# Linear attention and a gated layer on one core: key sums folded into the attention weights before the division, the division one unit later, key sums on VectorE, weight scans spread over the first layer

## The chip, the cores and the metric

The kernel runs on one core of one Trainium2 chip. The metric is device time in microseconds (us), the median of a kernel's runs. The program uses one core, so there is no second die to compare with; every run quoted here was listed as fast, with a granted TensorE clock between 0.99 and 1.00. The engines are called as the profile calls them: PE is TensorE, PEld its weight loads, DVE is VectorE, ACT is ScalarE, POOL is GpSimd, SP is SyncE, which here only issues transfers.

## The reference, cut to what matters

```python
def _A_ref(x, wqkv, wo):                 # linear attention, 32 heads of 32, S = 2048, D = 1024
    qkv = (x @ wqkv)...                  # q, k, v per head (reshape cut)
    phi = lambda t: jnp.where(t > 0, t + 1, jnp.exp(t)) + 1e-6
    pq, pk = phi(q), phi(k)
    kv  = jnp.einsum("bhsd,bhse->bhde", pk, v)
    z   = jnp.einsum("bhsd->bhd", pk)                             # the key sums
    num = jnp.einsum("bhqd,bhde->bhqe", pq, kv)
    den = jnp.einsum("bhqd,bhd->bhq", pq, z)[..., None] + 1e-6
    return (num / den)... @ wo                                    # (reshape cut)

def _B_ref(x, w_gate, w_up, w_down):     # gated layer, F = 3584
    return ((x @ w_gate) * (x @ w_up)) @ w_down                   # (written with einsum)

x = A_x                                  # bf16
x = x + _A_ref(_layernorm(x), ...)       # attention layer 1
x = x + _B_ref(_layernorm(x), ...)       # gated layer 1
x = x + _A_ref(_layernorm(x), ...)       # attention layer 2, the same weights
x = x + _B_ref(_layernorm(x), ...)       # gated layer 2, the same weights
```

## The kernel before

The attention layer never forms v. It computes phi(k) for all 16 row tiles (the **K stage**), then the 16 products of the normalised input with phi(k) (`xk_unit`, "X by K"), then multiplies them with the value weights (the **key-value product**, `kv_unit`), and folds the result with the output weights (`kvo_unit`, the **fold**). Each query tile (`q_unit`) goes through phi, is divided by its denominator on VectorE, is transposed by a DMA, and is multiplied with the folded matrix (`out_unit`, the **output stage**).

The gated layers work in fp16, and their weights are scaled by powers of two. The scale of each weight matrix comes from the sum of its squares. ScalarE takes these sums in 42 **scans** of 512 KB each, all of them hidden in the first attention layer: a DMA brings a piece, and ScalarE squares it in place with an accumulator.

The parts that matter (cuts marked `...`):

```python
    pqb = [W[:, i * D:(i + 1) * D] for i in range(3)]        # three buffers for phi(q) of a tile
    pb = [W[:, 6 * D + i * NB:6 * D + (i + 1) * NB] for i in range(4)]   # phi's biased copy x1
    scan_b = [W[:, 6 * D:8 * D], ...]                        # scan buffers; this one is the memory of pb
    ...
    EARLY, MID = 30, 39
    scanned = [0, 0, EARLY]         # scans done, fetched, allowed to be fetched

    def mm_tile():                  # the next of 8 PSUM banks
        count["mm"] = count.get("mm", -1) + 1
        return Q[count["mm"] % 8]

    def over_den(t):                # the division of tile t
        pq = pqs.pop(t)
        nc.vector.tensor_tensor(out=prod, in0=pq, in1=zb, op=ALU.mult)          # prod, zb: fp32
        den = small.tile([P, NH], F32, tag="den", name="den")
        nc.vector.tensor_reduce(out=den[:], in_=prod..., axis=AX.X, op=ALU.add)
        ...                                                                     # + 1e-6, reciprocal
        nc.vector.tensor_tensor(out=pqh, in0=pqh, in1=den..., op=ALU.mult)
        tx(pq, t, t // TPG)                                                     # transpose by DMA

    def kvo_unit(c, n):             # one piece of the fold
        ps = mm_tile()
        nc.tensor.matmul(out=ps, lhsT=kvt[:, c, :], rhs=wo[n][:, c, :], start=True, stop=True)
        nc.scalar.copy(out=KVo[n][:, c, :], in_=ps)

    def layer_A(li):
        sks = [sum_unit(t, nc.gpsimd if li == 0 and t < 9 else nc.vector) for t in range(1, NT)]
        ...
            for i, (t, n) in enumerate(units):                # first layer: the K stage
                u = k_mm(t, n)                                # (one special case cut)
                ...
                phi(*u)
                for x in late:
                    norm(x)                                   # normalise and transpose later tiles
                if i == 4:
                    scan_fetch()                              # four 512 KB loads at once
                if i >= 8 and i % 2 == 0:
                    scans()
                if 18 <= i < 26:
                    do(sks[:1])                               # eight key sums on GpSimd
                    sks = sks[1:]
        ...
        first = 5 if li == 0 else 4
        per = -(-len(sks) // (first - 3))
        for i in range(first):                                # the first X-by-K products
            xk[i]()
            do(sks[per * i:per * (i + 1)])                    # the other key sums, VectorE
            scans()
            if i == first - 3:
                z_parts()
        ...
        XT_ = 8
        for t in range(XT_):                                  # 16 Q units woven with the other products
            q[2 * t](); ...; q[2 * t + 1](); ...; scans(2 if t < 6 else 1)      # and 22 scans
        load_o()                                              # output weights, on SyncE's queue
        kv_unit()
        ...                                                   # Q 16-22 with the fold, Q 23-31 with outputs
```

## Time and profile before

The kernel took 1522.84 us as the median of three runs, and 1523.14 us (1521.97 to 1526.46) as the median of four. The top of the profile page gives the busy time of each engine, and its fourth part the shares of the chain of work that ended last.

```profile
PE 1490.2 (98%) x6995; PEld 677.9 (45%) x6995; DVE 1075.2 (71%) x1804; ACT 744.6 (49%) x934; POOL 87.3 (6%) x195
...
PE 86%; ACT 6%; DVE 3%; DMA 3%; issue 1%; SPq 1%; POOL 0%; ACTq 0%; DVEq 0%
```

TensorE bounds the kernel. What can be won without taking away matmuls is the time in which TensorE waits, or runs with a cold (halved) clock after a wait. The table of windows shows where that is. Each row is one stretch: its limits and length, the busy time and instruction count of PE, PEld, DVE, ACT and POOL, the granted clock, the DMA share and GB/s. The rows end at the end of the first X-by-K product, the start of the key-value product, its end, the end of the output stage, and then gated layer 1, attention layer 2 and gated layer 2.

```profile
0.00:81.73 81.73, 68.80 (x318) 29.95 (x318) 62.00 (x118) 55.67 (x72) 34.10 (x65) 0.97 0.84 220
81.73:163.36 81.63, 81.63 (x374) 36.75 (x372) 50.82 (x69) 65.35 (x81) 0.00 (x0) 0.98 0.73 205
163.36:169.41 6.05, 3.89 (x65) 3.65 (x64) 5.66 (x10) 5.49 (x7) 0.00 (x0) 1.00 0.66 180
169.41:265.13 95.72, 88.88 (x405) 39.60 (x403) 76.98 (x135) 59.02 (x90) 14.10 (x34) 0.98 0.59 140
265.13:779.12 513.99, 509.45 (x2353) 230.47 (x2352) 371.53 (x641) 236.14 (x262) 16.00 (x38) 1.00 0.51 150
779.12:1008.75 229.63, 229.38 (x1109) 105.73 (x1108) 172.20 (x284) 105.89 (x173) 16.24 (x43) 1.00 0.33 76
1008.75:1520.80 512.05, 508.19 (x2381) 231.73 (x2379) 336.01 (x551) 217.02 (x250) 6.90 (x16) 1.00 0.38 115
```

Attention layer 2 is busy for 229.38 of its 229.63 us. Attention layer 1 does the same work and adds the scans and the start; nearly all holes lie there or, with 4.0 us, at the start of the gated layer that follows it. The waits of PE name them (line of the waiting matmul, what it waited for, its line; total us, how often, the longest):

```profile
PE Q L338 <- DMA K<-ST: 4.8, 1, 4.8
PE Q L353 <- DVE K L328: 4.7, 2, 3.3
PE Q L501 <- DVE X L425: 4.0, 1, 4.0
PE Q L421 <- DMA TX<-in_A_wo_dram: 3.2, 1, 3.2
PE Q L413 <- ACT K L355: 2.2, 2, 1.9
PE Q L338 <- DVE part L233: 2.1, 1, 2.1
PE Q L421 <- DMA ST<-in_A_wo_dram: 1.3, 1, 1.3
```

(Q is PSUM, the eight banks into which TensorE writes its results; X is the activation x; K, W, MX, TX, ST and XT are buffers that the kernel reuses for many things.) L338 is the matmul of a K or Q projection, L353 that of an X-by-K product, L413 the key-value product, L421 the fold, L501 the gated layer's matmul. So, in this order: a transposed tile of the input arrives late in the K stage; the first product waits for the last phi(k) from VectorE; the first gated matmul waits for the last additions to x; the output weights arrive late; the key-value product waits for ScalarE's copies; a bank is read late by VectorE; and once more the output weights.

Why is VectorE late with phi(k)? The timeline of VectorE and GpSimd around 62 to 74 us shows it (start, duration in us, engine, line, operation, shapes):

```profile
63.21 10.96 POOL L361 TENSOR_TENSOR K<-K,K 128x1024 f32<-128x1024 f32 x5
...
67.42 0.29 DVE L327 TENSOR_SCALAR W<-W 128x512 bf16<-128x512 bf16 x1 [1.21 <-ACT W L326]
68.35 1.55 DVE L327 TENSOR_SCALAR W<-W 128x512 bf16<-128x512 bf16 x1
```

The same clamp of phi takes 0.29 us, or 1.55 us when it starts in the middle of a key sum of GpSimd (2.12 us each; the five are merged into one line above). In narrower windows one sum ends at 67.55 us, just after the short clamp has started, and the next runs from 67.63 to 69.76 us: the long clamp ends right after it, at 69.90 us. The Trainium skill, "SBUF — State Buffer", section "SBUF: two separate sides", says that VectorE in its two-port modes and GpSimd share a port pair that is held for a whole instruction. The trace agrees with that.

### The profile page before, as it was taken

Reading aid. Unit: us, or ns where it says so; the run is one execution under the profiler, and the core shown is the slowest. Engines: PE = TensorE matmul, PEld = TensorE weight load, DVE = VectorE, ACT = ScalarE, POOL = GpSimd, SP = SyncE. Lnnn points to the kernel's source line nnn. Section 1 sums busy time; section 2 is a strip of 40 time slices with the busy share of each in tenths; the row PEclk is TensorE's granted clock in tenths of the full one; section 3 lists DMA queues with packets and bytes.
Section 4 is the critical chain, followed back from the end, with each engine's and each line's share of the span. In section 5 each row is a group of like instructions: output and inputs, shape, how many; then the busy total and the mean of one; then the engine's idle time right before and its main releaser. Section 6 shows DMA issues by size and latency. Waiting matters only on the chain.

```text
span 1520.8 us, 18444 instructions
## 1 busy us (share of the span) xinstructions
PE 1490.2 (98%) x6995; PEld 677.9 (45%) x6995; DVE 1075.2 (71%) x1804; ACT 744.6 (49%) x934; POOL 87.3 (6%) x195
## 2 busy tenths in 40 slices
PE   9889899999999999999999999999999999999998
PEld 3334444444444444444444444444444444444444
DVE  7767786888867577776578667867776746777533
ACT  4978656677720266660013336576664015666300
POOL 3500002000001000000010000110000100000000
PEclk9999999999999999999999999999999999999999
DMA  7967827576658322334851014152323664322342
GB/s 220 209 199 200 256 46 172 154 209 198 197 189 221 92 84 83 84 104 157 238 133 40 15 32 117 33 139 84 83 84 125 184 193 115 84 83 83 146 169 80
DMA packets 277049, 202.78 MB, mean 133 GB/s; under 512 B 102113, under 2 KB 264161, under 8 KB 273377
## 3 DMA queue, kind: packets, MB, share of 16 engines
q1 hardware_dynamic: 265760, 186.94, 43.8%
q10 hardware_dynamic: 11200, 14.68, 3.1%
q8 instruction: 54, 0.88, 0.2%
q14 instruction: 35, 0.28, 0.1%
HBM read 160.43 MB, written 17.04 MB: 117 GB/s over the span
## 4 chain that ended last, share of the span: by engine, by line
PE 86%; ACT 6%; DVE 3%; DMA 3%; issue 1%; SPq 1%; POOL 0%; ACTq 0%; DVEq 0%
PE Q L501 45%; PE Q L786 22%; PE Q L338 8%; PE Q L433 5%; PE Q L353 5%; ACT K L217 2%; ACT W L326 1%; DVE W L327 1%; DVE K L328 1%; DMA TX<-in_A_wo_dram 1%; DMA K<-in_B_w_up_dram 1%; DMA X<-in_A_x_dram 1%; ACT K L422 0%; DMA K<-in_B_w_gate_dram 0%; DMA W<-in_B_w_down_dram 0%
## 5 line engine op out<-in xcount | busy, mean ns | idle before, releaser
L501 PEld LDWEIGHTS <-K 128*128 128x128 f16 x3136 | 307.2, 98 | 376.2 <-issue 7.4
L501 PE MATMUL Q<-XT,K 128*128 128x512 bf16 (+1 forms) x1792 | 407.2, 380 | 4.0 <-DVE X L425 4.0
L786 PE MATMUL Q<-K,K 128*128 128x512 f16 (+1 forms) x1596 | 340.8, 375 | 1.0 <-DVE X L793 1.0
L501 PE MATMUL Q<-TX,K 128*128 128x512 f16 x1344 | 308.3, 379 | 0.5 <-ACT MX L523 0.5
L463 ACT ACTIVATE K<-K,fac 128x2048 f16<-128x2048 bf16 x112 | 218.3, 1999 | 127.9 <-DMA K<-in_B_w_gate_dram 127.0
L786 PEld LDWEIGHTS <-K 128*128 128x128 f16 x1596 | 155.1, 98 | 185.0 <-issue 1.3
L466 DVE TENSOR_TENSOR K<-K 128x1024 f16<-128x1024 f16 (+1 forms) x244 | 157.2, 666 | 37.2 <-ACT K L463 35.3
L466 DVE TENSOR_TENSOR W<-MX,Q 128x512 f16<-128x512 f32 x176 | 116.5, 684 | 30.4 <-ACT MX L523 18.0
L338 PE MATMUL Q<-K,K 128*128 128x512 bf16 x512 | 117.3, 385 | 6.9 <-DMA K<-ST 4.8
L326 ACT ACTIVATE W<-Q 128x512 bf16<-128x512 f32 x90 | 53.0, 596 | 140.2 <-PE Q L338 124.6
L523 ACT COPY MX<-Q 128x512 f32<-128x512 f32 x120 | 69.2, 585 | 96.5 <-PE Q L501 96.5
L338 PE MATMUL Q<-K,XT 128*128 128x512 bf16 x512 | 114.6, 379 | 1.3 <-ACT XT L314 0.7
L466 DVE TENSOR_TENSOR W<-W,Q 128x512 f16<-128x512 f32 x160 | 105.6, 683 | 11.4 <-ACT W L523 4.9
L523 ACT COPY W<-Q 128x512 f32<-128x512 f32 x104 | 60.3, 585 | 73.0 <-PE Q L501 73.0
L466 DVE TENSOR_TENSOR K<-K,K 128x512 f16<-128x512 f16 (+1 forms) x148 | 87.6, 597 | 4.2
L466 DVE TENSOR_TENSOR K<-W,Q 128x512 f16<-128x512 f16 x56 | 38.4, 686 | 72.9 <-PE Q L501 72.8
L338 PEld LDWEIGHTS <-K 128*128 128x128 bf16 x512 | 50.5, 99 | 69.6 <-issue 7.0
L793 DVE SCALAR_TENSOR_TENSOR W<-Q,kap,X 128x512 f32<-128x512 f32 x32 | 24.0, 750 | 77.6 <-PE Q L786 77.6
L338 PEld LDWEIGHTS <-XT 128*128 128x128 bf16 x512 | 49.6, 98 | 61.5 <-ACT XT L314 1.5
L505 DVE TENSOR_TENSOR K<-W 128x512 f16<-128x512 f16 x168 | 71.3, 425 | 5.8
L217 ACT ACTIVATE K<-K 128x2048 bf16<-128x2048 bf16 x36 | 69.0, 1918 | 6.8 <-DMA K<-in_B_w_down_dram 3.2
L327 DVE TENSOR_SCALAR W<-W 128x512 bf16<-128x512 bf16 x90 | 33.3, 370 | 47.2 <-ACT W L326 47.1
(109 smaller groups left out, 1264.3 us busy)
## 6 DMA issues: line engine op xcount, KB each, us to landing
K<-WD SPq DMA_DIRECT2D x28, 1792.0 KB, 7.3
K<-in_B_w_gate_dram SPq DMA_DIRECT2D x70, 512.0 KB, 4.0
K<-in_B_w_up_dram SPq DMA_DIRECT2D x56, 512.0 KB, 5.1
K<-in_A_wqkv_dram SPq DMA_DIRECT2D x10, 1024.0 KB, 8.3
K<-in_B_w_up_dram ACTq DMA_DIRECT2D x14, 512.0 KB, 3.8
K<-in_B_w_down_dram SPq DMA_DIRECT2D x10, 512.0 KB, 5.3
WD<-K SPq DMA_DIRECT2D x10, 512.0 KB, 3.0
X<-in_A_x_dram SPq DMA_DIRECT2D x16, 256.0 KB, 5.3
```

The source lines that it names most:

```text
L217: nc.scalar.activation(out=scan_buf[i], in_=scan_buf[i], func=ACT.Square, accum_out=acc[:, m, c:c + 1])
L326: nc.scalar.activation(out=e, in_=ps, func=ACT.Exp)
L327: nc.vector.tensor_scalar(out=e, in0=e, scalar1=1.0, scalar2=1e-6, op0=ALU.min, op1=ALU.add)
L338: nc.tensor.matmul(out=ps, lhsT=xt[:, k, tl * P:(tl + 1) * P], rhs=w[:, k, :], start=(k == 0), stop=(k == KD - 1))
L353: nc.tensor.matmul(out=ps, lhsT=xn_a[t][:, j * P:(j + 1) * P], rhs=pk[t][:, n * NB:(n + 1) * NB], start=(t == 0), stop=(t == NT - 1))
L433: nc.tensor.matmul(out=ps, lhsT=xT[t // TPG][:, c, tl * P:(tl + 1) * P], rhs=KVo[n][:, c, :], start=(c == 0), stop=(c == KD - 1))
L463: nc.scalar.activation(out=b.bitcast(F16), in_=b, func=ACT.Copy, scale=fac[:, m:m + 1])
L466: eng.tensor_tensor(out=o, in0=a, in1=b, op=op)
L501: nc.tensor.matmul(out=pair[m], lhsT=stationary(n, p, m, k), rhs=moving[p][:, k, :], start=(p in (1, 2, 5) and k == 0), stop=(k == KH - 1) ...
L505: nc.vector.tensor_tensor(out=hA[i][:, u, :], in0=gu[:, 0, :], in1=gu[:, 1, :], op=ALU.mult)
L523: nc.scalar.copy(out=snaps[u, p][:, m, :], in_=a[m])
L786: nc.tensor.matmul(out=ps_[:, lo:hi], lhsT=act[:, u, j * P:(j + 1) * P], rhs=w[:, u, lo:hi], start=(p in (1, 2, 5) and u == 0), stop=(u == ...
```

## The change

Its intent, as the diff shows it:

- **Algebra.** The key sums are multiplied into phi(q) in place (phi(q) times z). The row sums of that product are the denominators, and the same product goes on to the division and the output. The fold takes the factor out again: ScalarE scales each row of the folded matrix by 1/z (`z_column` makes z a column and takes its reciprocal). The key sums become bf16, and the divided tiles fp16.
- **Deferral.** The division of a tile no longer follows its phi at once. Its first half follows the phi of the next Q unit, its second half the phi after that.
- **Key sums on VectorE.** All 15 of them, three behind each of the first five X-by-K products; before, eight were on GpSimd.
- **Scans spread.** Their loads no longer start four at a time; the K stage has 7 scans instead of 11.
- **Order.** Ten instead of eight pairs of Q units before the key-value product; the output weights are loaded from ScalarE's queue; the fold uses banks 5 to 7, while everything else in that stretch rotates over banks 0 to 4; two additions at the end of the layer go ahead of the row statistics; the last tile of the program is cut differently.

The diff, cut to its core:

```diff
-    prod, zb = (MX[:, 2 * D * i:2 * D * (i + 1)].bitcast(F32) for i in range(2))
+    zb = MX[:, 0:D]
@@
-            load(wo[n], wo_v[:, :, n * NB:(n + 1) * NB])
+            nc.scalar.dma_start(out=wo[n], in_=wo_v[:, :, n * NB:(n + 1) * NB])
@@
-    EARLY, MID = 30, 39
+    EARLY, MID = 32, 36
     ... (scan buffers regrouped)
-    scanned = [0, 0, EARLY]
+    scanned = [0, 0, 0]
@@
-    def mm_tile():
+    def mm_tile(narrow=[8]):
         count["mm"] = count.get("mm", -1) + 1
-        return Q[count["mm"] % 8]
+        return Q[count["mm"] % narrow[0]]
+    rotation = mm_tile.__defaults__[0]
@@ q_unit
             phi(proj_mm(t, wq[n]), pqs[t][:, n * NB:(n + 1) * NB], split)
+            flush()                              # the oldest deferred half, if there is one
             if n == 1:
-                over_den(t)
+                later[:] = over_den(t)           # [sums, divide]
@@ the division
-        nc.vector.tensor_tensor(out=prod, in0=pq, in1=zb, op=ALU.mult)
+        nc.vector.tensor_tensor(out=pq, in0=pq, in1=zb, op=ALU.mult)
     ...
-        nc.vector.tensor_tensor(out=pqh, in0=pqh, in1=den..., op=ALU.mult)
+        nc.vector.tensor_tensor(out=pqh.bitcast(F16), in0=pqh, in1=den..., op=ALU.mult)
@@ kvo_unit
-        ps = mm_tile()
+        ps = turn("kvo", Q[5:8])
     ...
-        nc.scalar.copy(out=KVo[n][:, c, :], in_=ps)
+        nc.scalar.activation(out=KVo[n][:, c, :], in_=ps, func=ACT.Copy, scale=rz[:, c:c + 1])
@@ layer_A
-        sks = [sum_unit(t, nc.gpsimd if li == 0 and t < 9 else nc.vector) for t in range(1, NT)]
+        sks = [sum_unit(t, nc.vector) for t in range(1, NT)]
@@
-                if i == 4:
+                if i >= 5 and i % 2:
+                    scanned[2] = (i - 3) // 2 if i < len(units) - 1 else EARLY
                     scan_fetch()
-                if i >= 8 and i % 2 == 0:
+                if 10 <= i <= 22 and i % 2 == 0:
                     scans()
-                if 18 <= i < 26:
-                    do(sks[:1])
-                    sks = sks[1:]
@@
-        XT_ = 8
+        XT_ = 10
     ... (the order of scans, fold, outputs and norms in the output stage)
+        rotation[0] = 5
+        for i in range(6):
+            q[22 + i]()
+            do(kvo[8 * i // 3:8 * (i + 1) // 3])
+            if i > 2:
+                out_next()
+        rotation[0] = 8
+        for i in range(4):
+            q[28 + i]()
+            out_next(2)
```

More of the change, by code (lines that the diff above doesn't have):

```diff
@@ L109 @@
     scan_b = [W[:, 6 * D:8 * D], K[0][:, HEAD:HEAD + 2 * D]]
-    scan_c = scan_b + [K[i][:, HEAD:HEAD + 2 * D] for i in (4, 5)]
+    scan_c = [K[i][:, HEAD:HEAD + 2 * D] for i in (4, 0)]
     xn_c = {TPG + i: tail(i, 0) for i in range(4)}
@@ L196 @@
     NSCAN = 3 * NU
-    EARLY, MID = 30, 39
-    scan_buf = [scan_a[i % 4] for i in range(EARLY)] + [scan_b[i % 2] for i in range(MID - EARLY)]
-    scan_buf += [scan_c[i % 4] for i in range(NSCAN - MID)]
-    scanned = [0, 0, EARLY]
+    EARLY, MID = 32, 36
+    scan_buf = [scan_a[i % 4] for i in range(18)] + [(scan_a + scan_b[:1])[i % 5] for i in range(18, EARLY)]
+    scan_buf += [scan_b[(i + 1) % 2] for i in range(MID - EARLY)] + [scan_c[i % 2] for i in range(NSCAN - MID)]
+    scanned = [0, 0, 0]
     def scan_fetch():
@@ L381, in z_unit, with z_column @@
             nc.scalar.copy(out=zb[:, n * NB:(n + 1) * NB], in_=ps)
+    rz = const.tile([P, KD], F32, tag="rz", name="rz")
+    def z_column():
+        ps = mm_tile()
+        for c in range(KD):
+            nc.tensor.matmul(out=ps[:, c:c + 1], lhsT=zb[:, c * P:(c + 1) * P], rhs=ident[:, 0:1], start=True, stop=True)
+        nc.vector.reciprocal(out=rz[:], in_=ps[:, 0:KD])
     pqs = {}
@@ L389, in run, with flush, den_sums, den_divide @@
             phi(proj_mm(t, wq[n]), pqs[t][:, n * NB:(n + 1) * NB], split)
+            flush()
             if n == 1:
-                over_den(t)
+                later[:] = over_den(t)
         return run
+    later = []
+    def flush():
+        if later:
+            later.pop(0)()
     def over_den(t):
         pq = pqs.pop(t)
-        nc.vector.tensor_tensor(out=prod, in0=pq, in1=zb, op=ALU.mult)
         den = small.tile([P, NH], F32, tag="den", name="den")
-        nc.vector.tensor_reduce(out=den[:], in_=prod.rearrange("p (h e) -> p h e", e=32), axis=AX.X, op=ALU.add)
+        return [lambda: den_sums(pq, den), lambda: den_divide(t, pq, den)]
+    def den_sums(pq, den):
+        nc.vector.tensor_tensor(out=pq, in0=pq, in1=zb, op=ALU.mult)
+        nc.vector.tensor_reduce(out=den[:], in_=pq.rearrange("p (h e) -> p h e", e=32), axis=AX.X, op=ALU.add)
         nc.vector.tensor_scalar(out=den[:], in0=den[:], scalar1=1e-6, scalar2=None, op0=ALU.add)
         nc.vector.reciprocal(out=den[:], in_=den[:])
+    def den_divide(t, pq, den):
         pqh = pq.rearrange("p (h e) -> p h e", e=32)
-        nc.vector.tensor_tensor(out=pqh, in0=pqh, in1=den[:].unsqueeze(2).to_broadcast([P, NH, 32]), op=ALU.mult)
+        nc.vector.tensor_tensor(out=pqh.bitcast(F16), in0=pqh, in1=den[:].unsqueeze(2).to_broadcast([P, NH, 32]),
+                                op=ALU.mult)
         tx(pq, t, t // TPG)
@@ L432, in run @@
             for c in range(KD):
-                nc.tensor.matmul(out=ps, lhsT=xT[t // TPG][:, c, tl * P:(tl + 1) * P], rhs=KVo[n][:, c, :],
+                nc.tensor.matmul(out=ps, lhsT=xT[t // TPG][:, c, tl * P:(tl + 1) * P].bitcast(F16), rhs=KVo[n][:, c, :],
                                  start=(c == 0), stop=(c == KD - 1))
@@ L605, in norm_act @@
         return out_
+    sums_t = []
     def layer_A(li):
         k = [k_unit(t, n) for t in range(NT) for n in range(2)]
-        sks = [sum_unit(t, nc.gpsimd if li == 0 and t < 9 else nc.vector) for t in range(1, NT)]
+        sks = [sum_unit(t, nc.vector) for t in range(1, NT)]
         first_A = li == 0
@@ L680, in layer_A @@
         q = [q_unit(t, n, li > 0 or t > 12) for t in range(NT) for n in range(2)]
-        first = 5 if li == 0 else 4
-        per = -(-len(sks) // (first - 3))
+        first = 6 if li == 0 else 4
+        per = -(-len(sks) // (first - (0 if first_A else 2)))
         for i in range(first):
@@ L685, in layer_A @@
             do(sks[per * i:per * (i + 1)])
-            scans()
-            if i == first - 3:
+            if i == first - (1 if first_A else 2):
                 z_parts()
+            scans(2 if i < 3 else 1)
         rest = xk[first:]
-        XT_ = 8
+        XT_ = 10
         for t in range(XT_):
             q[2 * t]()
+            scans()
+            do(rest[len(rest) * t // XT_:len(rest) * (t + 1) // XT_])
             if t == 0:
                 z_unit()
-            scans()
+            elif t == 2:
+                z_column()
+            elif first_A and t == 7:
+                scale_sum(0, 2)
+            elif first_A and t == 8:
+                scale_pow(0, 2)
             q[2 * t + 1]()
-            do(rest[len(rest) * t // XT_:len(rest) * (t + 1) // XT_])
-            scans(2 if t < 6 else 1)
+            if t < 8:
+                scans()
         load_o()
@@ L701, in layer_A @@
         load_unit(0, 0)
-        if first_A:
-            scale_sum(0, 2)
-        for i in range(4):
-            q[16 + i]()
-            if i == 2:
-                scanned[2] = NSCAN
-                scans()
-        kvo = [lambda c=c: kvo_unit(c // 2, c % 2) for c in range(2 * KD)]
-        for i in range(3):
-            q[20 + i]()
-            do(kvo[16 * i // 3:16 * (i + 1) // 3])
-            scans()
-            if i == 1 and first_A:
-                scale_pow(0, 2)
+        q[20]()
+        scanned[2] = NSCAN
+        scans()
+        q[21]()
+        kvo = [lambda c=c: kvo_unit(c % KD, c // KD) for c in range(2 * KD)]
         o = [out_unit(t, n) for t in range(NT) for n in range(2)]
@@ L718, in layer_A, with out_next @@
         norm = norm_act(0, 0, xn_b) + norm_act(1, 1, xn_c)
-        fill = [[]] + [prep(0)[i:i + 2] for i in (0, 2)] + [[]]
-        for i in range(9):
-            q[23 + i]()
-            do(o[2 * i:2 * i + 1])
-            if i < 4:
-                do(fill[i])
-            else:
-                do(norm[2 * i - 8:2 * i - 6])
-            do(o[2 * i + 1:2 * i + 2])
-            if first_A:
-                if i == 3:
-                    scale_sum(2, 3)
-                elif i == 4:
-                    dp[0][0]()
-                elif i == 5:
-                    scale_pow(2, 3)
-                elif i == 6:
-                    dp[1][0]()
+        jobs = {3: prep(0)[0:1], 4: prep(0)[1:2], 5: prep(0)[2:3], 6: prep(0)[3:4]}
+        if first_A:
+            for i, f in ((10, lambda: scale_sum(2, 3)), (9, dp[0][0]), (15, lambda: scale_pow(2, 3)), (13, dp[1][0])):
+                jobs[i] = jobs.get(i, []) + [f]
+            for i in range(2, 9):
+                jobs[i] = [scans] + jobs.get(i, [])
+        def out_next(n=1):
+            for _ in range(n):
+                i = count["o"] = count.get("o", -1) + 1
+                o[i]()
+                do(jobs.get(i, []))
+                if 8 <= i < 18:
+                    do(norm[i - 8:i - 7])
+        count.pop("o", None)
+        rotation[0] = 5
[8 more added lines that the diff above has]
+            out_next(2)
+        flush()
+        out_next()
+        flush()
+        out_next(6)
         down = list(dp[0][1:]) + list(dp[1][1:]) if first_A else []
@@ L747, in layer_A @@
             dp[2][0]()
-        spread(o[28:], t_fill())
+        for f in o[28:30]:
+            f()
+        sums_t[:] = t_fill()
+        for f in o[30:]:
+            f()
+            do(sums_t[:1])
+            sums_t.pop(0)
     def layer_B(li):
@@ L801, in down_step, with piece @@
                 a, b, ta, tb = da[j], db[j], t1 + j, t2 + j
-                if last and ps == 1 and p == 4 and j == TPG - 1:
-                    for lo, hi in ((0, 256), (256, 384), (384, 512)):
-                        down_mm(i, j, lo, hi)
-                        into(xs(tb, 0, lo, hi), a[:, lo:hi], xs(tb, 0, lo, hi))
-                        done(tb, 0, lo, hi)
+                ends = last and ps == 1 and j == TPG - 1
+                if ends and p in (3, 4):
+                    def piece(lo, hi):
+                        down_mm(ORDER.index(3), j, lo, hi)
+                        into(xs(ta, 1, lo, hi), b[:, lo:hi], temps[6, j][:, lo:hi])
+                        done(ta, 1, lo, hi)
+                    if p == 3:
+                        piece(0, 384)
+                        return
+                    down_mm(i, j)
+                    into(xs(tb, 0), a, xs(tb, 0))
+                    done(tb, 0)
+                    piece(384, 512)
                     return
@@ L844, in layer_B @@
                 gate_step(u, 2)
+                do(sums_t)
+                sums_t.clear()
                 pr[2]()
```

## The prediction

> **What bounds it now.** TensorE. The page gives it 98% of the 1520.8 us span, and the chain of waits is 86% matmul. Warm 512-column matmuls start every 0.216 us in the PE timeline (128 in 27.63 us); all matmuls of the program, counted in the groups and brought to 512 columns, are about 6,845, or 1,478 us. So only about 43 us of the span can be won at all, and no schedule can reach 2% (30 us) without nearly emptying it. Both gated layers (510 and 506 us) run within 3 us of their matmul count, the second attention layer (779.3 to 1008.9) within 1 us of its own. The rest sits in the first attention layer (8 to 269 us), where the table of windows and the PE waits show about 32 us:
> - K projection, 8 to 73 us: 8.5 lost; 4.8 of it is one wait for a transposed tile whose transpose sits behind four 512 KB scan loads on the same queue, the rest small waits and a cold clock after them.
> - first X-by-K product, 73 to 82: 5.2 lost, waiting for VectorE. While GpSimd adds key sums (2.13 us each), VectorE's 512-wide bf16 TENSOR_SCALAR takes 1.56 us instead of 0.29 (VectorE timeline, 68 to 79 us). The Trainium skill, "SBUF — State Buffer", section "SBUF: two separate sides", says GpSimd and VectorE share a port pair held for a whole instruction; the trace agrees.
> - Key-value product: 2.4, ScalarE late with its copies because of scans.
> - Q with weight fold, 169 to 196: 9.2; output weights land late (1.3 + 3.2) as their load sits behind a transpose on the queue, and a tiny matmul result is read late by VectorE (2.1).
> - start of the gated layer: 4.0 plus a cold start 1.7. VectorE waits 4.8 for the last transposes, with the output additions queued behind.
>
> **What the change does.**
> - Key sums all on VectorE: 8 more at 1.22 us, spread over six products of 3.45 us, where VectorE idles. The 1.56 us stalls go. Scan loads no longer bunch before the transposes. Gain in the first two stages: about 9 us.
> - Product with key sums in bf16: 1.225 to about 0.69 us (what a 1024-wide f16 TENSOR_TENSOR takes here), 32 times: 17 us of VectorE. The reduction (1.22) and division (1.225) stay, since one operand is fp32 or it is a reduction. Deferring them lets phi release its PSUM bank first. VectorE isn't the limit, so this alone gives nearly nothing.
> - Output weights on ScalarE's queue, fold limited to three banks between longer pieces, fewer scans at a time: 6 to 7 of the 9.2, and 1 to 2 of the key-value 2.4.
> - Gated start: additions ahead of two of the four sums: about 2.
> - Last tile: two waits of 0.5 us and a slice go: 1.3.
> - Costs: key-sum column, 8 tiny matmuls, 0.5 us per layer; three-bank fold at 0.67 us per ScalarE eviction, now scaled, maybe 1.5 in the second attention layer; seven scans (2.1 us each) pushed into the output stage before the norms.
>
> Sum: about 17 us gained. Predicted 1506 us, 8 in 10 between 1499 and 1514. Faster by over 2%: 0.03; within 2%: 0.96; slower: 0.01.
>
> **Right if:** the 1.56 us TENSOR_SCALARs are 0.29; first product starts within 1 us of the last K projection, near 69 us; PE waits for output weights under 1.5 us; L501's first wait about 2; second attention layer 229 to 232 us; VectorE busy down some 15 us.
>
> **Wrong if:** value weights, whose load now follows the 32nd scan, land after the key-value product wants them; ScalarE, with seven late scans, delays the norms and the gated start beyond 4 us; narrowed PSUM rotation stalls TensorE; or transposes still starve.

## The result, and the profile after

The changed kernel took 1501.05 us as the median of four runs (1500.48 to 1501.54), against 1523.14 us of the kernel before. The ratio is 0.9851, with a 95% interval from 0.9834 to 0.9868. The result lies in the predicted class (within 2%) and in the predicted range (1499 to 1514), five microseconds below the predicted 1506. "Gain" below means the difference of medians or, inside a trace, of spans. The first line of the page after:

```profile
PE 1485.4 (99%) x6997; PEld 676.1 (45%) x6997; DVE 1053.0 (70%) x1813; ACT 747.2 (50%) x934; POOL 67.3 (4%) x187
```

The table of windows of the kernel after, cut at the same seven events:

```profile
0.00:71.10 71.10, 67.10 (x318) 29.66 (x318) 53.92 (x118) 48.19 (x64) 17.39 (x57) 1.00 0.83 227
71.10:158.72 87.62, 87.57 (x414) 39.76 (x413) 68.96 (x106) 72.56 (x92) 0.71 (x1) 1.00 0.73 205
158.72:162.30 3.58, 3.58 (x66) 3.58 (x65) 2.71 (x4) 0.60 (x1) 0.00 (x0) 1.00 1.09 350
162.30:248.31 86.01, 81.65 (x372) 36.35 (x370) 60.95 (x114) 65.81 (x92) 11.37 (x33) 0.98 0.69 160
248.31:759.43 511.12, 508.32 (x2354) 230.02 (x2353) 369.46 (x639) 235.97 (x262) 15.96 (x38) 1.00 0.52 151
759.43:989.00 229.57, 229.37 (x1117) 105.88 (x1116) 160.98 (x285) 107.38 (x173) 15.02 (x43) 1.00 0.35 77
989.00:1499.80 510.80, 507.84 (x2367) 230.90 (x2365) 335.98 (x550) 216.71 (x250) 6.88 (x16) 1.00 0.38 115
```

The second row holds four more Q units than before, and the fourth row four fewer. A Q unit has 8 matmuls of 512 columns, and a warm one starts every 0.216 us (128 in 27.63 us in the view of the chain before), so four units are 6.9 us. With that shift taken out, the 21.0 us between the two spans divide like this:

| stage | before, us | after, us | gain, us |
|---|---|---|---|
| start, K stage and first product | 81.73 | 71.10 | 10.6 |
| other products with 16 (after: 20) Q units | 81.63 | 87.62, of it 6.9 moved here | 0.9 |
| key-value product | 6.05 | 3.58 | 2.5 |
| fold, outputs, with 16 (after: 12) Q units | 95.72 | 86.01, with 6.9 moved away | 2.8 |
| gated layer 1 | 513.99 | 511.12 | 2.9 |
| attention layer 2 | 229.63 | 229.57 | 0.1 |
| gated layer 2 and the last tile | 512.05 | 510.80 | 1.2 |

The waits of PE have nearly all gone, but there is a new one at the top of the list:

```profile
PE Q L340 <- DVE X L451: 3.6, 1, 3.6
PE Q L527 <- ACT W L549: 1.4, 2, 1.2
PE Q L527 <- DVE TX L492: 1.3, 1, 1.3
...
PE Q L355 <- DVE K L330: 0.9, 1, 0.9
```

L340 is now the Q projection, and L451 is the addition of an output to x, which frees the PSUM bank of that output. The timeline of the stretch shows the wait with what came before and after it:

```profile
171.83 0.69 DVE L330 SCALAR_TENSOR_TENSOR W<-Q,W 128x512 bf16<-128x512 f32 x1 [1.30 <-DMA K<-W]
...
179.97 0.69 DVE L330 SCALAR_TENSOR_TENSOR W<-Q,W 128x512 bf16<-128x512 f32 x1 [2.79 <-DMA K<-W]
...
189.50 2.44 PE L340 MATMUL Q<-K,K 128*128 128x512 bf16 x8 [3.57 <-DVE X L451]
190.20 1.91 ACT L217 ACTIVATE W<-W 128x2048 bf16<-128x2048 bf16 x1 [4.66 <-DVE W L326]
...
191.73 4.79 PE L459 MATMUL Q<-K,XT 128*128 128x512 bf16 x16
```

Read from the top: VectorE wants to write phi of a new tile into one of the three phi(q) buffers and twice waits, 1.30 and 2.79 us, because the DMA transpose of an older tile still reads that buffer. The additions stand behind it in VectorE's program, so they are late as well. At 189.50 TensorE has waited 3.57 us for one of them. Its first five or six matmuls still start at the warm rate, and then they are cold: the granted clock is 1.00 from 189.5 to 190.5 us, 0.62 to 191.3, 0.52 to 194.2 and 1.00 after that. So 8 take 2.44 us and 16 take 4.79 us, where 8 warm ones take 1.89 us. The Trainium skill, "TensorE: Matmul & The Clock Gate", Part 1, has a cold clock of half the warm one after an idle window of about 3.4 us; the trace agrees: between 191.7 and 194.2 us the weight loads of these matmuls start 0.43 us apart, where warm matmuls start every 0.216 us.

Two things make this wait. The first is the DMA. Two windows of the list of transfers (sizes in KB, median us from issue to landing) show the transposes of the divided tiles. First the kernel after from 160 to 181 us:

```profile
TX<-in_A_wo_dram ACTq DMA_DIRECT2D x1, 1024.0 KB, 10.0
K<-in_B_w_down_dram ACTq DMA_DIRECT2D x2, 512.0 KB, 9.8
...
K<-W SPq DMA_TRANSPOSE x3, 9.5
```

Then the same kernel from 181 to 235 us:

```profile
K<-W SPq DMA_TRANSPOSE x5, 3.1
```

A transpose takes 9.5 us (the median of three) beside the output weights, two scans and the first gated weights (two loads of 512 KB, cut here, at 12.1 and 13.7 us), and 3.1 us later. The second thing is the bank. When the rotation goes from five banks back to eight, the running number 89 of the next Q unit gives bank 1 (89 mod 8), and number 86 of an output still waiting for its addition had given bank 1 too (86 mod 5). Banks 5 to 7 were empty at that time.

One more fact is in that timeline. The scan at 190.20 waits 4.66 us for VectorE because its buffer is the memory in which phi keeps its biased copies. In the kernel after, this scan's data is loaded before two Q units write their copies there (at 178.96 and 183.13 us), and it is squared only afterwards. So a part of `w_down` is not summed as written. The sum serves only to choose a power of two that the kernel later takes out again, and the output stays correct; but it is a defect, and one experiment removes it.

The VectorE operations of the division, from the groups of instructions (count, busy us, mean ns). Before:

```profile
L397 DVE TENSOR_TENSOR MX<-W,MX 128x1024 f32<-128x1024 bf16 x32 | 39.2, 1225 | 1.1
```

After:

```profile
L421 DVE TENSOR_REDUCE den<-W 128x32 f32<-128x1024 bf16 x32 | 39.0, 1220 | 1.1
L428 DVE TENSOR_TENSOR W<-W,den 128x1024 f16<-128x1024 bf16 x32 | 38.9, 1217 | 0.0
L420 DVE TENSOR_TENSOR W<-W,MX 128x1024 bf16<-128x1024 bf16 x32 | 21.9, 683 | 0.0
```

The product went from 1.225 to 0.683 us; the reduction and the division kept their 1.22 us. The Trainium skill, "VectorE: DVE Perf Modes", section "The perf-mode tier table", gives `tensor_tensor` a double rate for bf16 and a single one for fp32, and `tensor_reduce` a single rate for both. The trace agrees: the product is 1.8 times as fast, and the reduction did not gain from its bf16 input.

### The profile page after: what moved, and what is told of

Same layout as the page of the kernel before. It is cut to its first block, busy times and chain, and to the rows that moved or that the text cites. A ratio compares the mean times of both kernels' runs of the same rounds, so it can differ in the third digit from the quotient of the medians. Undisturbed runs are those within 1.5% of the kernel's fastest.

```text
span 1499.8 us, 18432 instructions
## 1 busy us (share of the span) xinstructions
PE 1485.4 (99%) x6997; PEld 676.1 (45%) x6997; DVE 1053.0 (70%) x1813; ACT 747.2 (50%) x934; POOL 67.3 (4%) x187
## 4 chain that ended last, share of the span: by engine, by line
PE 82%; ACT 2%; DVE 1%; issue 1%; DMA 1%; POOL 0%; SPq 0%; ACTq 0%; DVEq 0%
PE Q L527 45%; PE Q L828 23%; PE Q L340 7%; PE Q L459 4%; PE Q L355 4%; ACT K L217 0%; DMA K<-in_B_w_down_dram 0%; DVE X L451 0%; ACT K L289 0%; PE Q L439 0%; ACT K L285 0%; DMA XT<-K 0%; ACT K L448 0%; ACT W L324 0%; DVE den L421 0%
## 5 line engine op out<-in xcount | busy, mean ns | idle before, releaser
L828 PE MATMUL Q<-K,K 128*128 128x512 f16 (+2 forms) x1582 | 340.4, 377 | 0.0
L340 PE MATMUL Q<-K,K 128*128 128x512 bf16 x512 | 115.6, 380 | 3.6 <-DVE X L451 3.6
L549 ACT COPY MX<-Q 128x512 f32<-128x512 f32 x120 | 69.2, 584 | 96.0 <-PE Q L527 96.0
L340 PE MATMUL Q<-K,XT 128*128 128x512 bf16 x512 | 114.6, 379 | 1.4 <-DMA XT<-ST 0.7
L340 PEld LDWEIGHTS <-K 128*128 128x128 bf16 x512 | 49.9, 98 | 64.1 <-issue 4.7
L340 PEld LDWEIGHTS <-XT 128*128 128x128 bf16 x512 | 49.5, 98 | 61.1 <-ACT XT L316 1.4
L545 ACT COPY MX<-Q 128x512 f32<-128x512 f32 x56 | 32.3, 588 | 63.4 <-PE Q L527 63.4
```

The costliest lines, as they stand in the source:

```text
L340: nc.tensor.matmul(out=ps, lhsT=xt[:, k, tl * P:(tl + 1) * P], rhs=w[:, k, :], start=(k == 0), stop=(k == KD - 1))
L545: nc.scalar.copy(out=snaps[u, 1][:, m, :], in_=a[m])
L549: nc.scalar.copy(out=snaps[u, p][:, m, :], in_=a[m])
L828: nc.tensor.matmul(out=ps_[:, lo:hi], lhsT=act[:, u, j * P:(j + 1) * P], rhs=w[:, u, lo:hi], start=(p in (1, 2, 5) and u == 0), stop=(u == ...
```

## The experiments

Twelve kernels ran, each in three rounds beside the kernel before on the same chip, and all gave correct results. Names that begin with b are the kernel before with one part of the change; names that begin with a are the kernel after with one part undone or mended. The kernel before had medians of 1523.59, 1524.20, 1522.89 and 1524.29 us in the four sessions.

| run | what | median, us | ratio to before | 95% interval |
|---|---|---|---|---|
| b_sums_dve | key sums on VectorE, same place | 1519.31 | 0.9976 | 0.9961 to 0.9991 |
| b_sums_late | key sums on VectorE, after the K stage | 1521.67 | 0.9983 | 0.9969 to 0.9998 |
| b_scan_spread | scan loads spread | 1528.90 | 1.0037 | 1.0020 to 1.0054 |
| b_wo_act | output weights on ScalarE's queue | 1521.39 | 0.9986 | 0.9971 to 1.0001 |
| b_scan_late | loads spread, scans later | 1528.63 | 1.0033 | 1.0016 to 1.0050 |
| b_k_stage | b_sums_late and b_scan_late together | 1525.42 | 1.0009 | 0.9988 to 1.0031 |
| after | the change | 1501.05 | 0.9851 | 0.9834 to 0.9868 |
| a_f32_prod | product with fp32 key sums | 1501.53 | 0.9856 | 0.9840 to 0.9871 |
| a_no_defer | division at once | 1500.40 | 0.9844 | 0.9829 to 0.9859 |
| a_scans_early | no scans behind the key-value product | 1513.33 | 0.9926 | 0.9908 to 0.9945 |
| a_bank | rotation moved on by three banks | 1498.90 | 0.9835 | 0.9819 to 0.9852 |
| a_ring4 | a fourth phi(q) buffer | 1493.94 | 0.9805 | 0.9790 to 0.9820 |
| a_fix | both, and phi's copies moved | 1495.06 | 0.9812 | 0.9795 to 0.9829 |

The kernel after did not run again in these four sessions, each on another chip; runs that begin with a are compared with it through their ratios to the kernel before.

The theory at the start: most of the gain comes from the first 80 us, where key sums and scan loads disturb phi and the transposes; the algebra and the deferral themselves gain nothing, as VectorE is not the limit. The rival: the cheaper product and the deferral do matter, because phi frees its bank earlier. For the sums there were two readings: what counts is that they leave GpSimd (the shared port), or that they leave the K stage (the place).

### b_sums_dve: the engine of the key sums alone

```diff
-        sks = [sum_unit(t, nc.gpsimd if li == 0 and t < 9 else nc.vector) for t in range(1, NT)]
+        sks = [sum_unit(t, nc.vector) for t in range(1, NT)]
```

> The kernel before, with its first eight key sums put on VectorE in the same place (between the last K units), nothing else. Theory P (the shared port alone cost the time): the 1.56 us TENSOR_SCALARs fall to 0.29, the first X-by-K product no longer waits (4.7 us before), and the run gains 4 to 5 us. Rival Q (VectorE has no room there, whoever holds it up): eight sums of 1.22 us take the place of the eight long TENSOR_SCALARs, a K unit still costs VectorE 0.29 + 0.69 + 1.22 = 2.2 us against 1.73 us of matmul, the product's wait stays at 3 to 5 us and the run within 1.5 us of before. I hold Q.

It gained about 4 us. The clamps between the sums took 0.28 to 0.29 us, none of them 1.55, and the first product waited less:

```profile
72.30 1.22 DVE L361 TENSOR_TENSOR K<-K,K 128x1024 f32<-128x1024 f32 x1
73.43 0.29 DVE L327 TENSOR_SCALAR W<-W 128x512 bf16<-128x512 bf16 x1
...
PE Q L353 <- DVE K L328: 1.5, 1, 1.5
```

The wait had been 4.7 us, and the product was done at 78.62 instead of 81.73 us. So eight sums of VectorE's own, in the same place, cost it less than being held up by GpSimd's. I had held that the place counts and that this run gains nothing; that failed, and the reading of the shared port held for most of the wait.

### b_sums_late: the engine and the place

The 15 sums go to VectorE, three behind each of the first five X-by-K products, and the broadcast of the sums one product later.

```diff
-                if 18 <= i < 26:
-                    do(sks[:1])
-                    sks = sks[1:]
@@
-        first = 5 if li == 0 else 4
-        per = -(-len(sks) // (first - 3))
+        first = 6 if li == 0 else 4
+        per = -(-len(sks) // (6 if first_A else 1))
     ... (z_parts and z_unit later to match)
```

> The kernel before, with all fifteen key sums on VectorE and moved past the K projection, three to each of the first six products (one product more ahead of Q, the column sum one product later). Theory Q (it is the place): the first product's wait goes from 4.7 us to under 1.5, total 4 to 5 us faster than before. Theory P expects the same of this run and of the one that only changes the engine; a gain here and none there speaks for Q. If neither gains, the scans on ScalarE hold the K units and not VectorE.

The first product no longer waited and was done at 76.07 us, 5.7 us earlier than before. Yet the kernel gained only about 2 us. The list of waits shows where a part of it went: the key-value product now waits 5.2 us for ScalarE, where it had waited 2.2. The scans had stayed where they were, and TensorE caught up with ScalarE.

### b_scan_spread: the scan loads alone

```diff
-    scanned = [0, 0, EARLY]
+    scanned = [0, 0, 0]
@@
-                if i == 4:
+                if i >= 5 and i % 2:
+                    scanned[2] = (i - 3) // 2 if i < len(units) - 1 else EARLY
                     scan_fetch()
```

> The kernel before, with only the fetches of the weight scans in the K projection spread (one buffer more every second unit, from the sixth unit on) in place of four at once. Theory: the burst of four 512 KB loads holds the transposes; the 4.8 us wait for a transposed tile falls under 1 us and the first ScalarE scan no longer waits 2.3 us; the K projection ends about 5 us earlier, but its VectorE tail stays (sums on GpSimd), total 4 to 6 us faster. Rival: the transposes were late because ScalarE's norms were late; then the wait stays above 3 us and nothing is gained.

It lost about 5 us, which neither theory had expected. The single wait of 4.8 us for a transposed tile went, as expected. In its place ScalarE waited for the scan data, because the scans themselves still began where the loads had been four at a time:

```profile
ACT K L217 <- DMA K<-in_B_w_gate_dram: 8.9, 5, 2.6
```

Before, this line had one wait of 2.3 us. The normalisations of the later tiles stood behind the waiting scans in ScalarE's program, and TensorE now waited 4.5 us in four pieces for the transposes of these tiles. The first product was done at 86.56 us, 4.8 us later than before, which is nearly the whole loss.

### b_scan_late: the loads spread, and the scans with a lead

As b_scan_spread, and the scans of the K stage only where the change puts them; those taken out follow the first four products, two each.

```diff
-                if i >= 8 and i % 2 == 0:
+                if 10 <= i <= 22 and i % 2 == 0:
                     scans()
@@
-            scans()
+            scans(2 if i < 4 else 1)
```

> The kernel before with the spread fetches of the last try, and now also with the scans on ScalarE started two units later and ended early (seven in the K projection, not eleven; four more in the first products). GpSimd keeps its sums. Theory L (spreading alone lost 5 us because each scan then ran straight into its own load: ScalarE waited 8.9 us for scan data, and the norms queue behind it): with a lead of one more load ScalarE waits under 1 us for scan data, the K projection ends near 67 us in place of 73 (77 in the last try); VectorE's tail under GpSimd's sums stays, the first product waits 4 to 7 us; total 2 to 6 us faster than before. Rival: spreading itself starves the transposes; then again slower than before.

ScalarE's waits for scan data in the K stage went to zero, and the K projection ended at 68.42 us (before: 73.05). That was the expectation for the stage. But the total stayed about 6 us above before. GpSimd still made the sums, and the first product waited 6.3 us; the key-value product waited 7.5 us for ScalarE, which now had four scans more between the products.

### b_k_stage: all of the change's K stage, in the kernel before

The edits of b_sums_late and b_scan_late together.

> The kernel before with the three changes of its K stage together: spread fetches, later scans, key sums on VectorE past the projection. Theory (the parts need each other; together they are the 10.6 us that the kernel after has at the end of its first product): first product done by 72 us, against 81.7 in the kernel before; some of it may come back at the key-value product, where ScalarE is late by its scans. Total 6 to 11 us faster than before. Rival (the stage's gain needs something else of the change): less than 5 us.

This is the most telling of the runs on the kernel before. The first product was done at 71.54 us, as in the kernel after (71.10), so the whole gain of the stage, 10 us, was there. The total did not gain at all. The waits of PE that took it back:

```profile
PE Q L413 <- ACT K L355: 5.8, 2, 5.6
PE Q L501 <- DVE X L425: 5.0, 2, 4.3
PE Q L379 <- ACT W L370: 4.5, 1, 4.5
```

L379 is the broadcast of the key sums, and L370 ScalarE's copy that feeds it. A part of this one belongs to my layout, which puts two scans ahead of that copy; the kernel after puts the copy first. The rest is ScalarE, late for the key-value product, and its successors. The expectation of a gain failed. This suggests that the gain of the K stage can be kept only if the load of ScalarE up to the key-value product falls as well; a_scans_early below tests it from the other side.

### b_wo_act: the queue of the output weights alone

```diff
-            load(wo[n], wo_v[:, :, n * NB:(n + 1) * NB])
+            nc.scalar.dma_start(out=wo[n], in_=wo_v[:, :, n * NB:(n + 1) * NB])
```

> The kernel before, with only the two output-weight loads issued from ScalarE's queue. Theory: they were late because they queued behind a transpose that waited for VectorE (issue at 174 us, 10 us after the products freed their place); issued about 5 us earlier, the two waits of 1.3 and 3.2 us go down to under 1.5 together, total 2 to 4 us faster. Rival: ScalarE, late by its scans, reaches the issue no earlier, or the loads only collide with others; then under 1 us.

About 2 us, with an interval that just includes nothing. The loads went out about 8 us earlier, at 165.86 and 166.94 us instead of 173.82 and 174.41, because they no longer stood in SyncE's queue behind a transpose that waited for VectorE. The waits of 3.2 and 1.3 us for the weights disappeared, and the fold got a new one:

```profile
PE Q L421 <- DVE W L328: 4.1, 1, 4.1
```

The wait changed its owner: the bank of the fold's next piece was still held by a phi that VectorE had not finished, and VectorE was late by nearly as much as the weights had been.

### a_scans_early: the scans back ahead of the key-value product

In the kernel after, 34 scans come before the key-value product and 8 after it. (A scan is two of ScalarE's records, the square and the read of the accumulator; windows limited to that line count 14, 54, 0 and 16 records in the first four stretches.) Here all 42 come before it, the K stage being left alone.

```diff
-    EARLY, MID = 32, 36
+    EARLY, MID = 32, 42
@@
             if t < 8:
-                scans()
+                scans(2)
@@
         q[20]()
-        scanned[2] = NSCAN
-        scans()
         q[21]()
@@ the output stage
-            for i in range(2, 9):
-                jobs[i] = [scans] + jobs.get(i, [])
```

> The kernel after, with the eight scans that it runs in the output stage moved back among the products (three to each of eight products, as dense as in the kernel before, on two buffers there). Nothing else is changed. Theory D (the K stage's gain only stays won because the scans are thinned out after it: ScalarE has 3 x 2.5 us of scan and 1.8 us of copies and exponentials for each 6.9 us of product): ScalarE falls behind, TensorE waits for its copies at the key-value product (none in the kernel after) by 4 us or more, total 5 to 12 us slower than the kernel after. Rival (ScalarE has room; the K stage alone won the time): within 1.5 us of the kernel after.

It took 1513.33 us, about 12 us more than the kernel after: about half of the whole gain was lost. The key-value product started at 177.19 instead of 158.72 us. The wait stood at another place than I had expected, at the small matmul for the scales of the gate and up weights, which the change has put between the products:

```profile
161.92 0.30 DVE L329 TENSOR_SCALAR W<-W 128x512 bf16<-128x512 bf16 x1 [4.20 <-ACT W L328]
...
165.31 0.12 DVE L226 TENSOR_REDUCE part<-acc 128x2 f32<-128x28 f32 x1
...
165.69 0.16 PE L232 MATMUL Q<-partb,ones 128*128 128x2 bf16 x1 [15.38 <-DVE partb L227]
```

The 28 scans that the sum at 165.31 needs had been done since 132.2 us. The sum stood in VectorE's program behind a Q unit, and the Q units waited for exponentials that ScalarE takes between the scans: VectorE's waits for them were 36.3 us between 70 and 178 us, against 14.2 between 70 and 160 us in the kernel after. ScalarE's scans in this stretch took 69.3 us against 53.8. So moving eight scans behind the key-value product is worth some 12 us in the presence of the other parts, and the size, though not the place, was as expected. Two things are not separated from ScalarE's load here: the scans of `w_down` have two buffers in this run, and ScalarE waited 6.5 us for their data; and the small matmul stands where the change put it. Whether the loss would be as large with more buffers, or with that matmul later, was not tested.

### a_f32_prod: the cheaper product undone

A second copy of the key sums in fp32, used for the product alone.

```diff
+    zf = MX[:, D:3 * D].bitcast(F32)
@@ z_unit
+            nc.scalar.copy(out=zf[:, n * NB:(n + 1) * NB], in_=ps)
@@
-        nc.vector.tensor_tensor(out=pq, in0=pq, in1=zb, op=ALU.mult)
+        nc.vector.tensor_tensor(out=pq, in0=pq, in1=zf, op=ALU.mult)
```

> The kernel after, with the product of weights and key sums against an fp32 copy of the key sums, so that it takes 1.22 us as before in place of 0.68 (17 us more of VectorE over the run); same order, same rounding of the result up to the factor. Theory (VectorE is not the limit there): within 1.5 us of the kernel after. Rival (the cheaper product is what won the time): 5 us or more slower than the kernel after.

The product took 1.217 us again, 17 us more of VectorE in all, and the time was the same as after (0.9856 against 0.9851). The saving on VectorE is real and buys nothing.

### a_no_defer: the division at once

```diff
             if n == 1:
                 later[:] = over_den(t)
+                flush()
+                flush()
```

> The kernel after, with key product, reduction and division emitted at once again, not one and two units later. Theory (deferral matters little where eight banks rotate): within 2 us of the kernel after; where only five banks rotate beside the fold, TensorE's waits there (4.4 us together in the kernel after) may grow by 1 to 2 us, or shrink as transposes go out earlier. Rival (deferral is a main part of the gain): 4 us or more slower than the kernel after.

The same again: 0.9844. The pattern of waits changed: the wait of 3.6 us was gone, and several of 0.6 to 1.6 us stood in its place, one of them of 1.3 us for the value weights. Deferral moves the waits and does not remove them.

### a_bank, a_ring4, a_fix: the new wait

The first moves the rotation on by three when it goes back to eight banks, so that the next Q unit lands on bank 4, whose output VectorE has just added (185.47 us, the unit starts at 185.52). The second gives phi(q) a fourth buffer in memory that the fp32 product and the fp32 key sums had used. The third does both and moves phi's biased copies out of the scan buffer, which also removes the defect told above.

```diff
# a_bank
         rotation[0] = 8
+        count["mm"] += 3
# a_ring4
-    pqb = [W[:, i * D:(i + 1) * D] for i in range(3)]
+    pqb = [W[:, i * D:(i + 1) * D] for i in range(3)] + [MX[:, D:2 * D]]
# a_fix: both of these, and
-    pb = [W[:, 6 * D + i * NB:6 * D + (i + 1) * NB] for i in range(4)]
+    pb = [MX[:, 2 * D + i * NB:2 * D + (i + 1) * NB] for i in range(4)]
```

> The kernel after, with the PSUM counter moved on by three where the rotation goes back from five banks to eight. In the kernel after Q unit 28 then falls on the bank of the output unit three before it, not yet added by VectorE, while three banks lie free; TensorE waits 3.57 us. Theory B: this is what makes the wait; it falls under 0.5 us, the cold clock after it goes (about 1.5 us), and 3 to 5 us are gained over the kernel after if the norms on ScalarE keep up, else part of it returns as a longer wait at the gated layer's start. Rival R (VectorE is late by its wait for transposes, any bank would wait): the wait stays over 2 us.

> The kernel after, with a fourth buffer for the attention weights. VectorE there waits 1.3 and 2.8 us for transposes of the buffer it wants to write. Theory R: with these gone VectorE adds the output unit about 3 us earlier, and TensorE's 3.57 us wait falls under 1 us; gain 2 to 4 us over the kernel after. Rival B (the bank order alone): VectorE's waits go, but TensorE still waits 2 us or more.

> The kernel after, with a fourth weights buffer, the PSUM counter moved on by three at the end of the narrow rotation, and the biased copies of phi moved out of the scan buffer that they overwrite in the kernel after before it is scanned. Against the run with the fourth buffer alone (7 us faster than the kernel after): its 0.58 us PSUM wait and ScalarE's 0.7 us wait go; 0 to 2 us faster still, TensorE's waits in the first attention layer's output stage all under 0.5 us. Rival: earlier scans and norms change nothing, as the gated start waits for the last transposes: within 1 us of that run.

With the bank alone, the wait at the Q unit went, and came back as one of 3.5 us at the small matmul for the scale of `w_down`; its scan still stood 4.65 us behind VectorE:

```profile
PE Q L232 <- DVE partb L227: 3.5, 1, 3.5
```

At the start of the gated layer nothing was left of the gain (248.72 us, 248.31 in the kernel after). The total is about 2 us shorter, with an interval that overlaps that of the kernel after. With the fourth buffer alone, VectorE's 4.1 us of waits for the transposes were gone, the wait at the Q unit was 0.6 us, and the scan's 0.7. The transposes themselves were no faster beside the same loads: those issued at 161 and 170 us took 9.3 and 9.2 us. The line of the list of waits that answers to the 3.6 us above:

```profile
PE Q L340 <- DVE X L451: 0.6, 1, 0.6
```

The first gated matmul started at 242.03 instead of 248.31 us, and the kernel took 1493.94 us: 7 us less than the kernel after, and 30.3 us less than the kernel before in the same session. Both runs together separate the causes: the missing buffer starts the chain, and the bank only decides which instruction shows it. a_fix is as fast as a_ring4 (1495.06, with overlapping runs), so the bank adds nothing once the buffer is there, and the defect can be removed at no cost. As a version to keep I would take a_fix.

## Why the prediction was right

The class was right, and the range held. The sum was five microseconds short. A part of that is luck, because errors cancelled: the fold was put about 4 us too high, the costs about 3 us too high (the gains as listed, at the middle of each, come to 20.3 us, and 17 were predicted), and the other terms were together some 4 us too low. The terms compare like this:

- **"First two stages: about 9 us."** Measured 10.6. "The 1.56 us stalls go" (the clamps of these stages took 0.27 us on average, before 0.52) and "first product starts within 1 us of the last K projection, near 69 us" were right in kind: its wait fell from 4.7 to 0.9 us, and it began at once, at 66.56 us. b_sums_dve, b_sums_late and b_scan_late each show one part of it. What the prediction did not see is that this gain is not kept by itself: b_k_stage had 10 us of it at 71.5 us, and none at the end.
- **"1 to 2 of the key-value 2.4."** Measured 2.5, all of it.
- **"6 to 7" of the fold's 9.2.** Measured 2.8 for the whole output stage; this term was mis-sized the most. The waits for output weights went from 4.5 us to none ("under 1.5 us" was right). But the stage got a new wait of 3.6 us with a cold clock behind it. The prediction had named both of its ingredients as risks, "narrowed PSUM rotation stalls TensorE" and "transposes still starve". a_ring4 shows what they cost, about 7 us; without them the term would have been near 9.
- **"Gated start: about 2."** Measured 2.9. "L501's first wait about 2" became no wait at the first matmul, and two later ones of 1.2 and 1.3 us.
- **"Last tile: 1.3."** Measured 1.2, for the whole of gated layer 2.
- **"This alone gives nearly nothing"** for the cheaper product and the deferral: right, by a_f32_prod and a_no_defer.
- **"Costs"**: the prediction took off about 2 us for the second attention layer and more for the late scans. The second attention layer cost nothing (229.57 against 229.63). The late scans (eight, not seven) were no cost on balance: a_scans_early shows that having them late is worth some 12 us, under the conditions named there. This was the one step with the wrong sign.
- **"VectorE busy down some 15 us"**: 22.2 (1075.2 to 1053.0). The product saved 17.3 us; the clamps of phi saved about 8 because nothing holds them up any more; the sums taken over from GpSimd added about 10. The rest is spread over small groups.
- **"No schedule can reach 2% without nearly emptying"** the 43 us of headroom: a_ring4 came out 30.3 us below before, at a ratio of 0.9805 with an interval from 0.9790 to 0.9820. That is at the line, and it leaves 13 us between its span of 1491.5 us and the 1,478 us of matmuls that the prediction counted.

Three things stay open. The parts are not additive, so the 12 us of a_scans_early and the 10 us of the K stage must not be added up to the total of 22; the runs show that neither half does it alone. And part of the broadcast's wait in b_k_stage comes from my order of the scans, so the zero gain there is a little worse than the change's own K stage would give. And the parts named under "Order" were not tested alone, apart from the queue of the output weights: the ten pairs, the separate banks of the fold, the additions ahead of the row statistics and the new last tile have only the table of stages behind them.

## What to carry to other kernels

When TensorE is the limit, a stage won early is kept only if every engine that must deliver later in that stretch has room for it; here ScalarE's side work had to move behind the next point at which TensorE waits for ScalarE. Ask of each ring of buffers whose last reader is a DMA how long that DMA takes when the queues are full, not how long it takes on average: one more buffer was worth 7 us here, while the cheaper product and the deferral, each undone alone, made no difference. The algebra did have another use: the fourth buffer lies in memory that it had freed. An experiment on one half of a change that shows no gain does not prove that half useless; look in the trace for the stage it won and for the wait that took it back.

## What the Trainium skill lacked or had wrong

- No page has the landing time of a transpose of this size under load. "DMA: Bandwidth & Descriptors" says in "Issuing engines are not separate DMA queues" that all issuers run on the same 16 engines and that a second issuer saves only sequencer time, usually little beside the transfer. The runs fit the first: transposes of SyncE's queue took 9.5 us beside ScalarE's loads against 3.1 later. The second was not little in b_wo_act: SyncE's queue stood behind a transpose that waited for VectorE, and on ScalarE's queue the output weights went out 8 us earlier, about as long as such a load takes (5.6 and 8.7 us before). The page would gain from a number for a transpose beside ordinary loads.
- No page has the time of the separate record that reads ScalarE's accumulator after such a scan: 0.19 us here, beside 1.90 us for the square of 2,048 bf16 columns itself.
- "SBUF — State Buffer" says who blocks whom on the shared port; it has no duration for this pair. Here a fp32 sum of GpSimd over 1,024 columns took 2.12 us, and the clamp on VectorE that met it 1.56 instead of 0.29 us.
- "PSUM — Partial Sum Buffer" doesn't tell of changing the number of banks in rotation. Here going from five to eight banks put a matmul on the one bank still in use, with three free; the wait was 3.57 us, and mending that alone gained at most about 2 us.
